# Slot sums for two sequences per matmul, and a reordered end of the token phase, in a recurrence-plus-soft-MoE kernel

## The chip, the cores and the metric

One core of a Trainium2 chip runs the whole program. Its engines work side by side, each on its own queue of instructions: TensorE (PE; its weight loads are shown as PEld) multiplies matrices into the accumulation memory (PSUM), VectorE (DVE) and ScalarE (ACT) work elementwise and copy out of PSUM, GpSimd (POOL) works elementwise on on-chip memory and issues the weight loads, and SyncE (SP) issues the other transfers. The metric is the device time of one execution in microseconds; lower is better. Times are given as the median of several executions.

## The reference

Four sequences of 5056 tokens with 256 channels go through a gated recurrence, and all 20224 tokens together through a soft mixture of eight experts with four slots each.

```python
# recurrence, per sequence
sig = 1.0 / (1.0 + np.exp(-f_logit))
f = lower_bound + (1.0 - lower_bound) * sig
h = f[:, t] * h + (1 - f[:, t]) * x[:, t]        # y[:, t] = h, for each t
# soft MoE over all tokens of all sequences, x = y
logits = x @ phi                                 # (20224, 32)
d = softmax of logits over the tokens
slot_input = d.T @ x                             # (32, 256)
h = np.maximum(slot_input[e] @ w1[e], 0.0)       # per expert e, its 4 slots
slot_out[e] = h @ w2[e]
c = softmax of logits over the 32 slots
out = c @ slot_out                               # (20224, 256)
```

The slot inputs need every token of every sequence, so no output can leave before the last token has been through the recurrence, the logits and the experts.

## The kernel before

**Token phase.** A sequence is cut into ten groups of up to 512 tokens (group 8, which the code calls `odd`, has 448; group 9 is `last`). One group of one sequence is a unit; there are 40, numbered n. For a unit, SyncE loads f_logit and x; ScalarE takes the sigmoid (`gate`, L249); GpSimd multiplies by x (`enter`, u_t, L260); TensorE transposes both to channels by rows (sp, up: L264, L271, L277, L300); ScalarE makes the decay (a, L315 and L322); VectorE scans along the tokens (h, L333); TensorE turns h back to tokens (`to_tokens`, hp, L346); and VectorE or ScalarE keeps that in ht (`keep_tokens`, L365). When all four sequences have a group, TensorE makes the logits (lg, L379), ScalarE their exponentials (`exps`, L388), TensorE transposes these (L400) and a copy keeps them as et (L403), and TensorE adds up the slot inputs (`slots`, L430).

**Slot sums.** The sums stand in one half of one PSUM bank, 128 partitions (4 sequences x 32 slots) by 256 channels. For a group, `slots` issues 16 matmuls (4 rows r x 4 sequences b), each with 32 columns of weights (et) and 256 moving columns (ht), and sequence b has its own 32 partitions. The sums for groups 0 to 7 are issued inside the loop, those for group 8 (L430) and group 9 (`late_slots`, L475) after it.

**Unread matmuls.** The other half of that bank takes `idle` matmuls (L194, in fp32, 128 columns of weights, 256 moving columns), issued at set places in the loop; nothing reads them. `spin` (L157) and `narrow` (L162, 32 columns of weights) are others, into other PSUM space, at the end of the token phase and among the experts.

**What sets the order.** The program's order is written by hand; every engine goes through its own instructions in that order. Waits between engines follow from the tiles: an instruction waits for the earlier instructions that wrote, or read, the tile it reads or writes. Transfers of experts' weights are issued on GpSimd's queue at set units (`W_AT`), the last six at n = 36; the w2 of the last two experts goes into a buffer (w_t, L152) that held f_logit.

**End of the token phase.** At n = 39 the logits of group 8 are finished for the last sequence, then come its exponentials, the slot sums of group 7, the transposes of group 8's weights (`odd_weights`, L469, copied by ScalarE, L470) and the scan of the last unit. After the loop: the last logits of group 9, `late_exps` (L454), hp and ht of the last unit, `late_weights` (L461, copied by VectorE, L462), the slot sums of groups 8 and 9, one copy of the sums to slot_sb (L614), and a matmul that adds the four sequences' 32 rows (L618). late_ps and odd_ps lie in one PSUM tile (tail).

**Experts and outputs.** The slot inputs go through w1 (L649), are turned (L664), and then through w2 (sum_ps, L688, for experts 0 to 6). Among experts 4 to 6 TensorE also adds each token's exponentials over the slots (`row_sums`, L413, into tail), whose reciprocals VectorE takes (rrow, L739). The last expert has its own form (so_ps, sb_ps, L748), and then slot_out (L760) is there and the output phase begins: matmuls (op, L788, L841), a scaled copy by VectorE or ScalarE (L778, L782), and stores.

Of the kernel before, what the change touches and what calls it, by code (L numbers as in the profile page):

```python
# [18 lines left out]
def kernel(  # L19
# [10 lines left out]
    nc = tc.nc  # L30
    B, S, D = x.shape
    E = moe_w1.shape[0]
    F = moe_w1.shape[2]
    NS = moe_phi.shape[1]
    SPE = NS // E
    P = 128
    DC = D // P
    FC = F // P
    R = 4
    G = P * R  # L40
    n_grp = (S + G - 1) // G
    n_unit = n_grp * B
# [12 lines left out]
    odd = n_grp - 2  # L55
# [12 lines left out]
    ident_f = consts.tile([P, P], F32, name="ident_f")  # L68
# [104 lines left out]
    with tc.tile_pool(name="sp2", bufs=3) as sp2, \  # L173
# [7 lines left out]
         tc.tile_pool(name="pslot", bufs=1, space=PSUM) as pslot:  # L181

        slot_bank = pslot.tile([P, 2, D], F32, name="slot_ps")
        slot_ps = slot_bank[:, 0]

        wide_rep = rep.rearrange("p b s -> p (b s)").unsqueeze(1).broadcast_to([P, 2, P])

        def idle(k, first=False):
            if first:
                for i in range(2):  # L190
                    nc.tensor.matmul(slot_bank[:, 1, ds(0, P)], ident, ident,
                                     start=True, stop=False, skip_group_check=True)
            for _ in range(k):
                nc.tensor.matmul(slot_bank[:, 1], ident_f, wide_rep,  # L194
                                 start=False, stop=False, skip_group_check=True)
        xs, fs, sts, uts, pss, psus, hs, hps, hts, lgs, ets = ({} for _ in range(11))

# [158 lines left out]
        def keep_tokens(n):  # L356
            g, b = place(n)
            n_p = rows(g)
            by_scalar = n % 2 and n >= SINGLE - 2
            if 2 * B < n < n_unit - 2 * B and n % (2 * B) in (1, B):  # L360
                by_scalar = not by_scalar
            if n in (n_unit - 8, n_unit - 4):
                by_scalar = True
            copy = nc.scalar.copy if by_scalar else nc.vector.tensor_copy
            copy(hts[g][:n_p, b].rearrange("p r d -> p (r d)").bitcast(F32),  # L365
                 hps.pop(n)[:n_p].rearrange("p r c -> p (r c)"))
# [58 lines left out]
        def slots(g):  # L425
            n_p = rows(g)
            et, ht = ets.pop(g), hts.pop(g)
            for r in range(R):
                for b in range(B):
                    nc.tensor.matmul(slot_ps[ds(b * NS, NS), :], et[:n_p, r, b],  # L430
                                     ht[:n_p, b, r],
                                     start=(g == 0 and r == 0),
                                     stop=(g == n_grp - 1 and r == R - 1),
                                     skip_group_check=True)

        def unit(f, m):
# [27 lines left out]
        def odd_weights():  # L464
            n_p = rows(odd)
            ets[odd] = etok.tile([P, R, B, NS], BF16, name="et", tag="et")
            ew = etall[:, ds(first(odd), n_p * R)].rearrange("s (p r) -> s p r", r=R)
            for r in range(R):
                nc.tensor.transpose(odd_ps[:n_p, r], ew[:, :, r], ident)  # L469
            nc.scalar.copy(ets[odd][:n_p].rearrange("p r b s -> p r (b s)"), odd_ps[:n_p])  # L470

        def late_slots():
            for r in range(R):
                for b in range(B):
                    nc.tensor.matmul(slot_ps[ds(b * NS, NS), :], ets[last][:, r, b],  # L475
                                     hts[last][:, b, r],
                                     start=False, stop=r == R - 1,
                                     skip_group_check=True)

        AHEAD = 6  # L480
        SETTLED = 3 * B
# [17 lines left out]
        for n in range(n_unit):  # L499
            if n < SINGLE - 2:  # L500
                if n:
                    unit(to_tokens, n - 1)
                    unit(u_to_channels, n + 1)
                s_to_channels(n + 2)
                if n + 3 < SINGLE:
                    gate(n + 3, 1)
                decay(n + 2, 1)
                if n + 3 == SINGLE:
                    gate(n + 3)
                if n % 2 == 0:  # L510
                    unit(load, n + AHEAD)
                unit(enter, n + 3)
                rep_constants(n)
            else:
                end = n >= n_unit - 6
                if n % 2 == 0:
                    unit(load, n + AHEAD)
                    if n == SINGLE - 2:
                        to_tokens(n - 1)
                        keep_tokens(n - 1)  # L520
                    if n >= SETTLED:
                        unit(gate, n + 4)
                else:
                    unit(decay, n + 1)
                    if seven(n) and place(n)[1] % 2 == 0:
                        nc.scalar.copy(uts[n + 2][:, R - 1], uts[n][:, R - 1])
                    if n < SETTLED:
                        gate(n + 3)
                    if n == n_unit - 5:
                        exps(odd - 1)  # L530
                if not end and n != n_unit - 7:
                    group(exps, n - 2)

                unit(enter, n + 3)
                for _ in range(W_AT.get(n, 0)):
                    load_w(w_next[0])
                    w_next[0] += 1

                late = seven(n)
                if n != SINGLE - 2 and not late:  # L540
                    unit(to_tokens, n - 1)
                if late:
                    unit(u_to_channels, n + 1)
                    unit(to_tokens, n - 1)
                if n == n_unit - 2:
                    keep_tokens(n - 1)
                if n % 2 == 0:
                    unit(s_to_channels, n + 2)
                    unit(s_to_channels, n + 3)
                if not late:  # L550
                    unit(u_to_channels, n + 1)
                if n == SINGLE - 2:
                    idle(1, True)
                elif late and n in (n_unit - 7, n_unit - 5, n_unit - 3):
                    idle(1)
                elif not late and n % (2 * B) in (1, 5, 6, 7):
                    idle(2 if n in (6, 7) else 1)
                if n == n_unit - 2:
                    tail = psp.tile([P, 2, G], F32, name="tail", tag="sp")
                    sums = tail[:, 0]  # L560
                    rs_ps = sums[:, ds(0, n_grp * R * B)].rearrange(
                        "p (q b) -> p q b", b=B)
                    late_ps, odd_ps = (
                        tail[:, 1].bitcast(BF16)[:, ds(i * R * P, R * P)].rearrange(
                            "p (r s) -> p r s", r=R) for i in range(2))
                    logits(odd, [0, 1, 2])
                    logits(last, [0, 1, 2])
                    slots(odd - 2)
                elif not end and long(n - 1):
                    if n % B == 0:  # L570
                        g = (n - 1) // (2 * B) * 2
                        for i in range(2):
                            logits(g + i, [2, 3] if n % (2 * B) == 0 else [0, 1])
                elif not end:
                    group(logits, n - 1)
            if n == n_unit - 1:
                logits(odd, [3])
                exps(odd)
                slots(odd - 1)
                odd_weights()  # L580

            unit(scan, n)
            if n not in (SINGLE - 2, n_unit - 2):
                unit(keep_tokens, n - 1)
            if n == n_unit - 3:
                weights_to_tokens(odd - 1, nc.scalar.copy)
            elif not n >= n_unit - 6:
                group(weights_to_tokens, n - 3)
                batch(slots, n - 4, 0)
                batch(slots, n - 4, 1)  # L590
                if n > 2 * B and n % (2 * B) == 3:
                    idle(1)
# [10 lines left out]
        late_exps()  # L603
        left_over()
        to_tokens(n_unit - 1)
        keep_tokens(n_unit - 1)
        late_weights()
        slots(odd)
        late_slots()
        spin(tail[:, 1], 2, D)  # L610
        narrow(tail[:, 1], 10)
        slot_sb = hpool.tile([P, G, DC], BF16, name="slot_sb", tag="h")
        slot_sb = slot_sb.rearrange("p t o -> p (t o)").bitcast(F32)[:, ds(0, D)]
        nc.vector.tensor_copy(slot_sb, slot_ps)  # L614
        sin_ps = tail[:, 0, ds(G // 2, DC * NS)].rearrange("p (o s) -> p o s", o=DC)
        slot_v = slot_sb.rearrange("p (c o) -> p o c", o=DC)
        for o in range(DC):
# [5 lines left out]
    with tc.tile_pool(name="ew", bufs=1) as ew, \  # L623
# [108 lines left out]
        for i in range(len(blocks)):  # L732
            expert(Q + i)
            row_sums(i)
            if i < 2:
                narrow(tail[:, 1], 34, NS)
            if i < len(blocks) - 1:
                k = ds(i * wide_r, wide_r)
                nc.vector.reciprocal(rrow[:, k], rs_ps[:, k])  # L739
# [166 lines left out]
```

## Time and profile before

| | |
|---|---|
| Time, median of 3 runs | 198.06 us (198.0 to 199.38) |
| The profiled execution's own time | 197.88 us |
| Its span, first to last instruction | 196.1 us |
| Mean TensorE clock granted | 0.877 of full speed |
| TensorE busy | 150.4 us (77%), 1328 matmuls |
| VectorE busy | 144.2 us (74%) |
| ScalarE busy | 142.6 us (73%) |
| GpSimd busy | 101.2 us (52%) |
| HBM read, written | 58.23 MB, 20.71 MB |

The profile comes from one execution. Its page cuts the span into 40 equal slices (4.9 us each) and gives, for each, the busy share of each engine in tenths, the granted TensorE clock in tenths and the share of the 16 DMA engines. A timeline row reads: start in us from the span's beginning, duration, engine, line, operation, what is written and read, shapes (rows*columns of the array in use, then partitions x elements), how many in a row, and in brackets how long the engine had been idle and what released it. Rows of a chain of waits are pieces of the path that ended last: start, duration, engine, tile and line. Matmuls are pipelined, so the durations of neighbours overlap, and a row of several is shorter than their sum.

### The profile page before, as it was taken

To read this page: it belongs to the slowest core of one execution; us is meant where nothing else is said; L and a number is where in the kernel's file an instruction comes from. 1 tells how busy PE (TensorE), PEld (TensorE's weight loads), DVE (VectorE), ACT (ScalarE), POOL (GpSimd) and SP (SyncE) were. 2 spreads that over 40 slices of the span, in tenths; PEclk is the share of its full clock that TensorE was granted. 3 is DMA by queue.
4 is the path that set the end of the run, shared out by engine and by line. 5 is a ranking of instruction groups with operands and counts; after the bars stand their busy time and mean duration, and the time that the engine had idled before them with its cause. 6 is when DMAs were issued, how large, how long until landed. Compare 5 with 4: busy or idle time off the path is not lost.

```text
span 196.1 us, 3514 instructions
## 1 busy us (share of the span) xinstructions
PE 150.4 (77%) x1328; PEld 104.7 (53%) x1328; DVE 144.2 (74%) x187; ACT 142.6 (73%) x202; POOL 101.2 (52%) x78
## 2 busy tenths in 40 slices
PE   0687579888979979897999998999899999930000
PEld 0475458676756858665786776648674434300000
DVE  3669789999899999999989999333377998920000
ACT  3688678899689999899986898425089999950000
POOL 2689586894988588894989995270030000000000
PEclk9999999999999999999999999999995555555555
DMA  5999999999999999999999999999749999999994
GB/s 209 419 419 419 433 428 423 428 424 340 399 424 421 398 346 423 428 424 322 407 422 409 241 212 215 214 215 211 133 166 428 420 434 424 428 434 438 448 434 177
DMA packets 13010, 70.77 MB, mean 361 GB/s; under 512 B 1457, under 2 KB 2738, under 8 KB 9026
## 3 DMA queue, kind: packets, MB, share of 16 engines
q1 hardware_dynamic: 10368, 62.13, 76.0%
q0 software_dynamic: 2624, 8.42, 21.6%
q8 instruction: 10, 0.16, 0.3%
q14 instruction: 6, 0.05, 0.1%
q10 hardware_dynamic: 2, 0.00, 0.0%
HBM read 58.23 MB, written 20.71 MB: 403 GB/s over the span
## 4 chain that ended last, share of the span: by engine, by line
PE 39%; DMA 22%; DVE 13%; ACT 7%; POOL 5%; issue 3%; POOLq 1%; ACTq 0%; SPq 0%
DMA x_t<-in_x_dram 14%; DVE h L333 9%; PE op L841 9%; DMA f_t<-in_f_logit_dram 7%; PE hp L346 5%; PE up L271 5%; POOL u_t L260 4%; ACT oc L782 3%; PE sp L264 2%; PE sp L271 2%; DVE ht L365 2%; PE lg L379 2%; PE op L788 2%; PE slot_ps L194 2%; PE tail L413 1%
## 5 line engine op out<-in xcount | busy, mean ns | idle before, releaser
L260 POOL TENSOR_TENSOR u_t<-s_t,x_t 128x1024 bf16<-128x1024 bf16 (+1 forms) x39 | 82.4, 2127 | 20.7 <-ACT s_t L249 11.3
L333 DVE TENSOR_TENSOR_SCAN h<-a,h,up 128x512 bf16<-128x512 f32 (+1 forms) x72 | 86.6, 1251 | 3.6 <-PE up L271 2.5
L249 ACT ACTIVATE s_t<-f_t 128x2048 bf16<-128x2048 f32 (+2 forms) x23 | 38.3, 1669 | 7.0 <-DMA f_t<-in_f_logit_dram 7.0
L346 PE MATMUL hp<-ident_f,h 128*128 128x128 f32 (+1 forms) x160 | 29.0, 304 | 5.8 <-DVE ht L365 3.9
L346 PEld LDWEIGHTS hp<-ident_f,h 128*128 128x128 f32 (+1 forms) x160 | 23.1, 206 | 13.9 <-DVE ht L365 7.8
L315 ACT ACTIVATE a<-sp,lbs 128x1024 f32<-128x1024 bf16 x24 | 25.4, 1114 | 0.6 <-PE sp L264 0.6
L271 PE MATMUL up<-ident_f,u_t 64*128 64x64 f32 x248 | 23.1, 229 | 2.7 <-POOL u_t L260 2.5
L782 ACT ACTIVATE oc<-op,rrow 128x256 f32<-128x256 f32 x62 | 24.4, 508 | 0.2
L264 PE MATMUL sp<-ident_f,s_t 128*128 128x128 f32 x128 | 19.1, 292 | 6.8 <-ACT s_t L249 4.5
L841 PE MATMUL op<-slot_bd,etall 64*128 64x512 bf16 x62 | 23.3, 584 | 0.5 <-POOL slot_bd L771 0.3
L271 PEld LDWEIGHTS up<-ident_f,u_t 64*128 64x128 f32 x248 | 18.1, 138 | 7.9 <-POOL u_t L260 3.4
L322 ACT ACTIVATE a<-sp,lbs 128x512 f32<-128x512 bf16 (+1 forms) x22 | 18.2, 875 | 5.4 <-PE sp L264 3.1
L778 DVE TENSOR_TENSOR oc<-op,rrow 128x512 f32<-128x512 f32 x31 | 19.9, 684 | 1.9 <-PE op L841 1.9
L264 PEld LDWEIGHTS sp<-ident_f,s_t 128*128 128x128 f32 x128 | 15.3, 150 | 8.7 <-ACT s_t L249 5.0
L194 PE MATMUL slot_ps<-rep,ident_f 128*128 128x256 f32 x48 | 15.7, 416 | 1.0 <-POOL rep L88 1.0
L841 PEld LDWEIGHTS <-etall 64*128 64x128 bf16 x62 | 9.0, 153 | 13.4 <-issue 7.9
L365 DVE COPY ht<-hp 128x512 f32<-128x512 f32 (+1 forms) x20 | 13.4, 671 | 2.2 <-PE hp L346 2.2
L365 ACT COPY ht<-hp 128x512 f32<-128x512 f32 (+1 forms) x20 | 11.7, 583 | 2.8 <-PE hp L346 2.8
L333 DVE TENSOR_TENSOR_SCAN h<-a,up 128x512 bf16<-128x512 f32 x8 | 9.3, 1208 | 2.5 <-ACT a L322 1.7
L379 PE MATMUL lg<-h,phi 128*32 128x512 bf16 (+1 forms) x80 | 10.1, 390 | 0.0
L194 PEld LDWEIGHTS slot_ps<-rep,ident_f 128*128 128x128 f32 x48 | 7.3, 188 | 2.8 <-POOL rep L88 1.2
L430 PE MATMUL slot_ps<-ht,et 128*32 128x256 bf16 (+1 forms) x144 | 8.6, 276 | 0.0
(131 smaller groups left out, 147.7 us busy)
## 6 DMA issues: line engine op xcount, KB each, us to landing
f_t<-in_f_logit_dram SPq DMA_DIRECT2D x12, 1024.0 KB, 13.0
x_t<-in_x_dram SPq DMA_DIRECT2D x12, 1024.0 KB, 12.1
out_dram<-oc SPq DMA_DIRECT2D x6, 2048.0 KB, 13.5
w_sb<-in_moe_w_dram POOLq DMA_DIRECT2D x14, 512.0 KB, 10.4
f_t<-in_f_logit_dram SPq DMA_DIRECT2D x8, 512.0 KB, 9.2
x_t<-in_x_dram SPq DMA_DIRECT2D x8, 512.0 KB, 8.8
f_t<-in_f_logit_dram SPq DMA_DIRECT2D x4, 896.0 KB, 13.0
x_t<-in_x_dram SPq DMA_DIRECT2D x4, 896.0 KB, 11.7
```

The costliest lines, as they stand in the source:

```text
L194: nc.tensor.matmul(slot_bank[:, 1], ident_f, wide_rep, start=False, stop=False, skip_group_check=True)
L249: nc.scalar.activation(s_t, f_t, ACT.Sigmoid, scale=-1.0)
L260: nc.gpsimd.tensor_tensor(uts[n][:, :r], s_t[:, :r], x_t[:, :r], ALU.mult)
L264: nc.tensor.transpose(ps[:, :, r], t(n % 2 * R + r).bitcast(F32), ident_f)
L271: nc.tensor.transpose(v[:, :, r], t(r)[k].bitcast(F32), ident_f[k, k])
L315: nc.scalar.activation(a, sp[:, :, :, :, o], ACT.Identity, scale=nomlb[:, ds(o, 1)], bias=1.0)
L333: nc.vector.tensor_tensor_scan(h[:, :T, o], decays[n // 2, o][:, n % 2, :T], up[:, :T, o], hs[number(g - 1, b)][:, ds(used(g - 1) - 1, 1), ...
L346: nc.tensor.transpose(hp[:n_p, r], hw[:, :n_p, r], ident_f)
L365: copy(hts[g][:n_p, b].rearrange("p r d -> p (r d)").bitcast(F32), hps.pop(n)[:n_p].rearrange("p r c -> p (r c)"))
L778: nc.vector.tensor_tensor(ob, op, scale.broadcast_to(list(ob.shape)), ALU.mult)
L782: nc.scalar.activation(ob[:, i], op[:, i], ACT.Copy, scale=scale[:, i])
L841: nc.tensor.matmul(op.rearrange("p u d -> p (u d)"), ew[:, :, r], slot_bd[ds(j * 2 * NS, 2 * NS)].rearrange("s u d -> s (u d)"), start=Tru ...
```

## The change

`slots` takes two sequences at once for groups 0 to 6: 64 columns of weights (the et of both) and 512 moving columns (the ht of both), eight matmuls a group instead of 16. The output fills 64 partitions by the whole bank. The blocks on the diagonal are the sums wanted (an even sequence in the first half of the bank, an odd one in the second); the other two blocks mix two sequences and aren't read. Groups 7, 8 and 9 still take one sequence at a time, into the half that belongs to it. `late_slots` is replaced by `slots(last)`, which does the same work.

Since the bank is now full, `idle` writes only a block that isn't read, 32 partitions of the second half: it has 32 columns of weights instead of 128. The three idle matmuls at n = 33, 35 and 37 go. The sums are copied to slot_sb in four pieces of 32 partitions, by VectorE and ScalarE in turn, each from the half that holds its sequence.

`odd_weights` moves from n = 39 to behind `to_tokens` of the last unit, so the last logits come ahead of it on TensorE, and `late_exps` ahead of its copy on ScalarE. The last unit's ht copy goes from ScalarE to VectorE. The two runs of 34 `narrow` matmuls among the experts go. No transfer changes, and GpSimd's and SyncE's queues keep their order.

```diff
         slot_bank = pslot.tile([P, 2, D], F32, name="slot_ps")
-        slot_ps = slot_bank[:, 0]
...
-                    nc.tensor.matmul(slot_bank[:, 1, ds(0, P)], ident, ident,
+                    nc.tensor.matmul(slot_bank[ds(0, NS), 1, ds(0, P)], ident[:, ds(0, NS)], ident,
                                      start=True, stop=False, skip_group_check=True)
             for _ in range(k):
-                nc.tensor.matmul(slot_bank[:, 1], ident_f, wide_rep,
+                nc.tensor.matmul(slot_bank[ds(0, NS), 1], ident_f[:, ds(0, NS)], wide_rep,
                                  start=False, stop=False, skip_group_check=True)
...
             if n in (n_unit - 8, n_unit - 4):
                 by_scalar = True
+            if n == n_unit - 1:
+                by_scalar = False
...
         def slots(g):
             n_p = rows(g)
             et, ht = ets.pop(g), hts.pop(g)
+            k = 2 if g < odd - 1 else 1
             for r in range(R):
-                for b in range(B):
-                    nc.tensor.matmul(slot_ps[ds(b * NS, NS), :], et[:n_p, r, b],
-                                     ht[:n_p, b, r],
-                                     start=(g == 0 and r == 0),
-                                     stop=(g == n_grp - 1 and r == R - 1),
+                for b in range(0, B, k):
+                    dst = slot_bank if k == 2 else slot_bank[:, b % 2]
+                    nc.tensor.matmul(dst[ds(b * NS, k * NS)],
+                                     et[:n_p, r, ds(b, k)].rearrange("p b s -> p (b s)"),
+                                     ht[:n_p, ds(b, k), r] if k == 2 else ht[:n_p, b, r],
+                                     start=g == 0 and r == 0,
+                                     stop=g == n_grp - 1 and r == R - 1,
                                      skip_group_check=True)
...
-        def late_slots():
-            for r in range(R):
-                for b in range(B):
-                    nc.tensor.matmul(slot_ps[ds(b * NS, NS), :], ets[last][:, r, b],
-                                     hts[last][:, b, r],
-                                     start=False, stop=r == R - 1,
-                                     skip_group_check=True)
...
-                elif late and n in (n_unit - 7, n_unit - 5, n_unit - 3):
-                    idle(1)
                 elif not late and n % (2 * B) in (1, 5, 6, 7):
                     idle(2 if n in (6, 7) else 1)
...
                 exps(odd)
                 slots(odd - 1)
-                odd_weights()
...
         to_tokens(n_unit - 1)
+        odd_weights()
         keep_tokens(n_unit - 1)
         late_weights()
         slots(odd)
-        late_slots()
+        slots(last)
...
-        nc.vector.tensor_copy(slot_sb, slot_ps)
+        for b in range(B):
+            k = ds(b * NS, NS)
+            (nc.scalar.copy if b % 2 else nc.vector.tensor_copy)(slot_sb[k], slot_bank[k, b % 2])
...
             row_sums(i)
-            if i < 2:
-                narrow(tail[:, 1], 34, NS)
```

## The prediction

> **What bounds the kernel now.** I began with the page's 40 slices: which resource never rests, and where it does.
>
> ```profile
> PEclk9999999999999999999999999999995555555555
> DMA  5999999999999999999999999999749999999994
> ```
>
> The DMA engines are full from the first loads to slice 27 and again from slice 30; the clock falls to half only with the outputs. Between 140 and 145 us DMA rests (share 0.37 in 140 to 142, 0.11 in 142 to 145). So the time is: loads and weights until about 142, a gap, then 20.71 MB of outputs at about 430 GB/s, 48 us that nothing shortens. What counts is when the first output leaves, and that needs the last expert's w2 and the slot sums. The timeline there, and the issues of that w2 (tile w_t, POOL's queue):
>
> ```profile
> 119.64 0.54 POOL L152 DMA_DIRECT2D w_t<-in_moe_w_dram  x1 [0.43 <-DMA w_sb<-in_moe_w_dram]
> 127.06 0.53 POOL L152 DMA_DIRECT2D w_t<-in_moe_w_dram  x1 [1.91 <-DMA w_sb<-in_moe_w_dram]
> ...
> 141.41 0.60 PE L748 MATMUL so_ps<-w_t,hid 128*128 128x256 bf16 x4
> 141.94 0.11 PEld L748 LDWEIGHTS <-hid 128*128 128x128 bf16 x2 [0.22 <-DMA w_t<-in_moe_w_dram]
> ```
>
> Four issues take 15.5 to 19.4 us to land: the 256 KB part 122.10 + 19.3 = 141.4, the last 128 KB 127.06 + 15.5 = 142.6. TensorE starts L748 at 141.41 and waits again at 141.94. Its weights for L748 were loaded from 141.17, so it stands ready some 0.1 us before the part. Compute and weights finish together: **work taken out ahead of L748 can gain almost nothing, work put in is paid in full** once some 0.2 us of waiting (0.1 here, 0.1 at 141.94) is used up.
>
> Next, the chain of waits back from there. From 56 us it is compute, changing between VectorE's scans and stretches of TensorE; these pieces (start, us) are touched:
>
> ```profile
> 75.45 0.63 PE slot_ps L194 x2
> 76.08 0.47 PE hp L346 x4
> ...
> 96.31 0.54 PE slot_ps L430 x11
> 96.84 0.68 PE hp L346 x4
> ...
> 122.59 0.54 PE slot_ps L430 x12
> ```
>
> L430 is a slot sum of a group, L194 an idle matmul.
>
> **The change part by part**, on the profiled run's own 197.88 us (span 196.1; the median of the three runs is 198.06, 0.2 above).
>
> *Pairs, groups 0 to 6.* Sixteen 32-column, 256-wide matmuls become eight 64-column, 512-wide. The sixteen took 0.53 to 0.55 us on the chain, so four quarters of the array run at once. Eight on two halves are four waves of 512; the logits, also 512 wide and two abreast there, go at 0.23 a wave (chain, 73.13 and 73.37). 4 x 0.23 = 0.92, so +0.38 a group. Groups 0, 1, 2 and 4 run where TensorE then waits for VectorE or loads (after 68.6 it waits until 70.3), so those are covered; without that cover they cost 0.38 each. Groups 3, 5 and 6 (73.6, 96.3, 122.6) are on the chain: **+1.15**. No 64-column matmul is in this trace. Bounds: 0 if it goes as before; if halves don't overlap, a 512-wide one after another costs 0.25 (L841, 1.72 for 7 at 145.58), 8 x 0.25 - 0.55 = +1.4 a group, 4.3 in all. I take the waves, since every 32-column group here overlaps.
>
> *Idle matmuls with 32 columns.* Streaming stays 256 wide. But hp, 0.47 after L194, is 0.68 after L430 or the 64-row transposes: a change of tile shape costs 0.2. The narrow idle brings that change. Three lie on the chain (58.0, 75.5, 98.2): **+0.6**. Below, shorter weight loads (0.11 between its two loads) could give back 0.1 each, -0.3; above, a second change, +1.2. The nearest row is hp's. [...]
>
> *Three late idles gone.* At 109.0 the transposes behind it wait for ScalarE's u_t copy (109.09 to 109.49); at 113.4 ScalarE is busy from 112.74 to 117.2 and sets the pace; at 118.4 TensorE waits afterwards until 120.12. All beside the path: 0 (bounds -1.2, thrice 0.43, to 0).
>
> *Group 8's weights later.* The tail of before:
>
> ```profile
> 125.01 0.63 PE L469 MATMUL tail<-ident,etall 128*112 128x128 bf16 x4 [0.29 <-ACT etall L388]
> 125.57 0.62 PE L379 MATMUL lg<-h,phi 128*32 128x512 bf16 x2
> 125.67 0.59 ACT L470 COPY et<-tail 112x512 bf16<-112x512 bf16 x1 [0.72 <-PE tail L469]
> 126.12 0.75 PE L346 MATMUL hp<-ident_f,h 128*128 128x128 f32 x4
> 126.23 0.60 ACT L454 ACTIVATE etall<-lg 128x512 bf16<-128x512 f32 x1
> 126.97 0.41 PE L461 MATMUL tail<-ident,etall 128*128 128x128 bf16 x4
> 128.65 0.42 DVE L614 COPY slot_sb<-slot_ps 128x256 f32<-128x256 f32 x1 [0.73 <-PE slot_ps L475]
> 129.28 0.55 PEld L618 LDWEIGHTS tail<-rep,slot_sb 128*128 128x128 f32 x4 [0.21 <-DVE slot_sb L614]
> ```
>
> In the changed program the last logits wait for group 8's exponentials (one lg tile), and group 9's transposes wait for ScalarE's copy of group 8's (one tail tile). So: exponentials done 124.96; logits 125.0; hp 0.55 later, 125.56; group 8's transposes 0.68 later, 126.24, about 0.5; copy 126.8 to 127.4; group 9's transposes 127.4 instead of 126.97. **+0.4**: the logits gain 0.55 and the copy that had been beside them moves onto the path. The last ht copy, 0.6 on ScalarE, goes to VectorE (0.69 for such a copy) at about 126.35, ahead of its next work: covered; uncovered 0.1. Behind the waiting transposes stand both groups' slot sums and all that follows. If the tile waits cost nothing, -0.55; above, +0.6.
>
> *Four copies of slot_sb.* 32 rows by 256 each, VectorE and ScalarE in turn, and in the built program each waits for the one before, the matmul L618 for the last. A 32x256 VectorE copy took 0.40 (L717), a 128x256 ScalarE one 0.41 (L756): rows fewer, no time saved. 0.06 + 0.42 + 0.41 + 0.42 + 0.41 + three hand-overs of 0.04 + 0.05 = 1.89 from the last slot sum (128.59) to L618; it was 0.69. **+1.2**. Bounds: 0.25 each (L630's 128x32) +0.5; ScalarE at 0.76 (L700, 32x256) +1.9.
>
> *No unread matmuls among experts.*
>
> ```profile
> 135.98 1.22 PE L413 MATMUL tail<-ones,etall 128*128 128x128 bf16 x16
> 137.12 0.41 PE L162 MATMUL tail<-w_sb 128*32 128x32 bf16 x34
> 137.62 0.56 DVE L739 RECIPROCAL rrow<-tail 128x64 f32<-128x64 f32 x1 [2.46 <-PE tail L162]
> ```
>
> The reciprocal waits for the 34, and the next row sums (138.23) for the reciprocal. Without them it starts at 137.27 and the row sums at 137.88: -0.35, twice, **-0.7** (bounds -0.8, the 0.41s, to 0).
>
> Sum at L748: 1.15 + 0.6 + 0.4 + 1.2 - 0.7 = 2.65, less the 0.2 of waiting: +2.45. SP's and POOL's queues keep their order; loads land about 12 us after issue, so DMA doesn't starve meanwhile. **197.88 + 2.45 = 200.3 us.**
>
> **Rivals.** *Not slower: the last w2 stays late.* Decided at L748: while compute is under 0.2 us later there, 142.6 still sets the end. It needs VectorE to cover the pairs and shape changes (it is 90% busy or more in most slices from 12 to 22) and copies of 32 rows at L630's 0.25: 0.4 + 0.5 - 0.7 = 0.2, so 197.9. Against it: the chain names TensorE at those places, and L717. Up to 198.9 if part holds. Faster than that it can't be; the weights land when they land.
>
> *The clock drops before the outputs.* Mean clock is 0.79 in 145 to 150, with TensorE busy 4.51 of 5.00 us, and 0.50 in 150 to 155, busy 5.00: being busy doesn't hold it. There the matmuls use 64 or 32 rows. If the used area counts, idles with a quarter of the columns hold it less, as do late idles and experts' fillers left out. L841 went from 0.25 to 0.43 us each, so a TensorE stretch like 120.1 to 124.3 would take 2 to 3 us more: about 202.5, up to 205 with two. For it: so many fillers are cut at once. Against: from 120 to 142, mostly 32-column work, clock 1.00, and the pairs double the area. [...]
>
> *Halves that don't overlap*: 4.3 for 1.15, 203.4.
>
> **How the numbers follow.** Forecast 0.45 (199.4 to 201.2), not slower 0.21, clock 0.20, no overlap 0.14. The range 198.4 to 203.4 leaves about 0.1 below and 0.1 above: the bounds of the copies and shapes move the end by under 1, those of the pairs make the last rival. 1% (2 us) is about what this kernel's measurement tells from no change; over 200.04 lie two thirds of the forecast and both dear rivals: slower 0.62, same 0.34, faster 0.04.
>
> **What would show it.** Four slot_sb copies in a row, 1.7 us or more; slot sums of 0.9 us; group 9's transposes over 2 us after group 8's exponentials; L748 reached after w2 has landed, with no wait for DMA; outputs as full as now. I am wrong if a wait for w_t still stands before L748, or if PEclk shows less than full before slice 30.

## The result and the profile after

The changed kernel takes **204.36 us** (median of four executions, 202.44 to 204.59) against 198.13 us for the kernel before on the same chip: a ratio of 1.0279, 95% interval 1.0203 to 1.0354. Measured once more beside another set of executions of the kernel before, it took 202.94 us against 199.06, ratio 1.0209 (1.0127 to 1.0291). The forecast was 200.3 us. The profiled execution took 204.15 us, with a span of 202.4 us, 6.3 longer than before. In the page's 40 slices (5.06 us each; the granted clock, then the DMA share):

```profile
PEclk9999669996999999999999995899999655555555
DMA  6999999999999999999999999999019999999994
```

Before, the clock was full in every slice up to the outputs. Here it is at half in three more places: 21.8 to 28.7 us (slices 4 and 5), 45.7 to 49.2 (slice 9) and 120.8 to 127.7 (slices 23 to 25). DMA rests longer ahead of the outputs: two slices at 0 and 1 tenth, where before the lowest were 7 and 4.

The end of the token phase and the first matmuls on w2, from the timeline:

```profile
134.61 0.41 DVE L610 COPY slot_sb<-slot_ps 32x256 f32<-32x256 f32 x1 [0.73 <-PE slot_ps L433]
135.06 0.36 ACT L610 COPY slot_sb<-slot_ps 32x256 f32<-32x256 f32 x1 [2.14 <-DVE slot_sb L610]
135.45 0.42 DVE L610 COPY slot_sb<-slot_ps 32x256 f32<-32x256 f32 x1 [0.43 <-ACT slot_sb L610]
135.91 0.36 ACT L610 COPY slot_sb<-slot_ps 32x256 f32<-32x256 f32 x1 [0.49 <-DVE slot_sb L610]
136.32 0.55 PEld L614 LDWEIGHTS tail<-rep,slot_sb 128*128 128x128 f32 x4 [1.28 <-ACT slot_sb L610]
...
147.68 0.60 PE L742 MATMUL so_ps<-w_t,hid 128*128 128x256 bf16 x4
```

The four copies stand one behind the other. L742 (L748 before; line numbers shift by up to six between the two kernels) begins at 147.68, 6.27 us later than before, and carries no wait: the last w2 landed at 143.4. So compute sets the end, as the forecast had it, and the 6.3 us of the span are all there before the first output.

Pieces of the chain of waits (start, us, what; L433 is a slot sum here, L193 an idle matmul, L345 hp):

```profile
46.44 1.85 PE slot_ps L433 x8
48.29 0.99 PE slot_ps L193 x2
...
75.85 0.98 PE slot_ps L433 x8
76.84 0.68 PE hp L345 x4
...
78.15 0.55 PE slot_ps L193 x2
78.70 0.68 PE hp L345 x4
```

Eight paired matmuls take 0.98 us at full clock (sixteen single ones took 0.54) and 1.85 at half. After an idle, hp now takes 0.68 instead of 0.47, while the idle (L193) takes 0.55 instead of 0.63.

### The profile page after: what moved, and what is told of

Same layout as the page of the kernel before. It is cut to its first block, busy times and chain, and to the rows that moved or that the text cites. A ratio compares the mean times of both kernels' runs of the same rounds, so it can differ in the third digit from the quotient of the medians.

```text
span 202.4 us, 3257 instructions
## 1 busy us (share of the span) xinstructions
PE 157.0 (78%) x1198; PEld 102.4 (51%) x1198; DVE 144.9 (72%) x189; ACT 142.6 (70%) x203; POOL 101.3 (50%) x78
## 4 chain that ended last, share of the span: by engine, by line
PE 43%; DVE 15%; DMA 10%; ACT 10%; POOL 6%; issue 3%; SPq 1%; POOLq 1%; ACTq 0%
DVE h L332 10%; PE op L835 8%; PE hp L345 7%; DMA x_t<-in_x_dram 7%; PE up L270 5%; POOL u_t L259 5%; ACT oc L776 5%; PE sp L263 4%; PE slot_ps L433 4%; DMA f_t<-in_f_logit_dram 3%; PE lg L380 3%; DVE ht L366 3%; PE sp L270 2%; ACT a L321 2%; PE slot_ps L193 2%
## 5 line engine op out<-in xcount | busy, mean ns | idle before, releaser
L248 ACT ACTIVATE s_t<-f_t 128x2048 bf16<-128x2048 f32 (+2 forms) x23 | 38.3, 1669 | 3.3 <-DMA f_t<-in_f_logit_dram 3.3
L345 PE MATMUL hp<-ident_f,h 128*128 128x128 f32 (+1 forms) x160 | 31.0, 320 | 4.6 <-DVE ht L366 4.1
L345 PEld LDWEIGHTS hp<-ident_f,h 128*128 128x128 f32 (+1 forms) x160 | 23.0, 208 | 18.2 <-DVE ht L366 9.5
L263 PE MATMUL sp<-ident_f,s_t 128*128 128x128 f32 x128 | 20.0, 302 | 6.6 <-ACT s_t L248 4.4
L776 ACT ACTIVATE oc<-op,rrow 128x256 f32<-128x256 f32 x62 | 24.3, 540 | 0.2
L835 PE MATMUL op<-slot_bd,etall 64*128 64x512 bf16 x62 | 22.7, 570 | 0.6 <-ACT oc L776 0.2
L263 PEld LDWEIGHTS sp<-ident_f,s_t 128*128 128x128 f32 x128 | 16.3, 156 | 8.3 <-ACT s_t L248 4.7
L366 DVE COPY ht<-hp 128x512 f32<-128x512 f32 (+1 forms) x21 | 14.1, 672 | 5.5 <-PE hp L345 5.5
L366 ACT COPY ht<-hp 128x512 f32<-128x512 f32 (+1 forms) x19 | 11.1, 585 | 8.4 <-PE hp L345 8.4
L193 PE MATMUL slot_ps<-rep,ident_f 128*32 128x256 f32 x42 | 13.5, 413 | 0.0
L380 PE MATMUL lg<-h,phi 128*32 128x512 bf16 (+1 forms) x80 | 12.1, 443 | 0.3 <-ACT etall L389 0.3
L433 PE MATMUL slot_ps<-ht,et 128*64 128x512 bf16 (+2 forms) x104 | 10.5, 353 | 0.0
L765 POOL TENSOR_SCALAR slot_bd<-slot_out,parity 128x256 bf16<-128x256 bf16 x2 | 1.8, 918 | 16.7 <-DVE slot_out L754 16.7
```

Of the source, the lines that this page charges most:

```text
L248: nc.scalar.activation(s_t, f_t, ACT.Sigmoid, scale=-1.0)
L263: nc.tensor.transpose(ps[:, :, r], t(n % 2 * R + r).bitcast(F32), ident_f)
L345: nc.tensor.transpose(hp[:n_p, r], hw[:, :n_p, r], ident_f)
L776: nc.scalar.activation(ob[:, i], op[:, i], ACT.Copy, scale=scale[:, i])
L835: nc.tensor.matmul(op.rearrange("p u d -> p (u d)"), ew[:, :, r], slot_bd[ds(j * 2 * NS, 2 * NS)].rearrange("s u d -> s (u d)"), start=Tru ...
```

## The experiments

Fifteen more runs were made, two of them of the unchanged kernels. Each is compared with executions of the kernel before on its own chip in the same session; over all sessions those took 197.9 to 201.1 us, with medians from 198.0 to 199.3. That spread is itself a finding, below. "Early drop" is half clock before 60 us, "late drop" half clock between 118 and 128 us. All these kernels compute the whole reference.

| kernel | median us | beside it, before | ratio (95%) | half clock in its profile, ahead of the outputs |
|---|---|---|---|---|
| before, again | 198.96 | 198.92 | 1.0001 (0.9966 to 1.0037) | 22.5-26.0, 118.1-121.5 |
| before, 32-column idles | 198.98 | 199.32 | 1.000 (0.996 to 1.004) | 22.7-26.1 |
| before, no late idles | 201.42 | 199.32 | 1.011 (1.004 to 1.018) | 22.7-26.1, 118.3-125.1 |
| before, only n = 33, 35 | 201.06 | 198.40 | 1.0145 (1.0077 to 1.0213) | 22.8-26.2, 118.3-125.2 |
| before, only n = 37 | 199.74 | 198.40 | 1.0061 (1.0014 to 1.0108) | 45.0-48.5 |
| before, no narrow | 199.32 | 199.32 | 0.9992 (0.996 to 1.0024) | 21.6-28.5, 45.5-48.9 |
| before, four copies | 199.74 | 199.06 | 1.0039 (0.9997 to 1.0081) | 22.9-26.4 |
| before, late idles doubled | 198.68 | 199.06 | 0.9986 (0.995 to 1.0021) | 21.9-28.8, 45.8-49.3 |
| before, more idles | 199.68 | 199.06 | 1.0026 (0.999 to 1.0061) | 58.2-61.7 |
| after, again | 202.94 | 199.06 | 1.0209 (1.0127 to 1.0291) | 23.7-27.2, 119.3-126.1 |
| after, late idles back | 201.35 | 198.92 | 1.0146 (1.0088 to 1.0204) | 24.0-27.5 |
| after, only n = 37 back | 202.26 | 197.99 | 1.0204 (1.0139 to 1.0268) | 22.8-26.3 |
| after, quadrant idles | 203.19 | 199.32 | 1.0187 (1.0107 to 1.0267) | 34.9-38.3 |
| after, no pairs | 199.88, the others 203.21 to 203.34 | 198.92 | none | 24.5-31.4, 120.1-126.9 |
| after, no pairs, late idles back | 200.10 | 198.92 | 1.0073 (1.0043 to 1.0103) | 24.3-27.8 |

The first theory was that the clock fell because the idles use a quarter of the columns, early and late alike. The next four sections test it.

### The kernel before with narrow idles

```diff
-                nc.tensor.matmul(slot_bank[:, 1], ident_f, wide_rep,
+                nc.tensor.matmul(slot_bank[ds(0, NS), 1], ident_f[:, ds(0, NS)], wide_rep,
```

> The kernel before, with one part of the change: the idle matmuls have 32 columns of weights and write 32 partitions; all of them stay, the three at n = 33, 35, 37 too. Theory 1 (the width of the idles decides the clock early): the granted clock shows less than full near 22 to 29 us and 46 to 49 us, as in the changed kernel, and the time is 2.0 to 2.6 us over the kernel before (there the scan's h at 60.7 us came 2.26 later). Rival (the early drops came from the pairs or by chance of phase): the clock stays full up to the outputs, and the time is 0.3 to 0.6 us over, for the changes of tile shape alone. If the late idles too need their width, a drop near 120 us comes on top: 3.5 to 4.5 over.

Measured: 198.98 against 199.32 us, ratio 1.000 (0.996 to 1.004). Its clock:

```profile
PEclk9999889999999999999999999999996555555555
```

One short early drop, and full from 26.1 us to the outputs. Theory 1 falls at its centre: the width of the idles costs no time that shows, and doesn't make the late drop.

### The kernel before without the late idles

```diff
-                elif late and n in (n_unit - 7, n_unit - 5, n_unit - 3):
-                    idle(1)
```

> The kernel before without the three idle matmuls at n = 33, 35 and 37; nothing else. Theory 1 (they hold the clock over the end of the token phase): the clock drops to half near 117 to 124 us for some 7 us, and the time is 1.5 to 2 us over the kernel before (hp, lg and the last slot sums at half clock lost about 1.7 in the changed kernel). Rival (they lay beside the path and hold nothing; the late drop follows from the narrow idles before): full clock, time within 0.2.

Measured: 201.42 us, 2.1 over the kernel before beside it (by the interval 0.8 to 3.6). Its clock:

```profile
PEclk9999789999999999999999985999995555555555
```

The late drop is there, 118.3 to 125.1 us, with nothing changed but three matmuls of 0.4 to 0.6 us that nobody reads. This part of the theory stands.

### The changed kernel with idles that fill the array

```diff
+            for _ in range(4 * k):
+                for b in range(B):
+                    nc.tensor.matmul(slot_bank[ds(b * NS, NS), 1 - b % 2], ident[:, ds(0, NS)],
+                                     wide_id, start=False, stop=False, skip_group_check=True)
...
+                elif late and n in (n_unit - 7, n_unit - 5, n_unit - 3):
+                    idle(1)
```

> The changed kernel, with idles that fill the array again: each idle is four rounds of four bf16 matmuls of 32 columns and 256 moving, one for each block of the bank that is not read, so all 128 columns are in use for about as long; and the three idles at n = 33, 35, 37 are back. Pairs, four copies, reordered end and no narrow matmuls among the experts stay. Theory 1 (used columns of the idles hold the clock): full clock up to the outputs, and the time falls from 204.2 to 199.9 to 200.6 us, the forecast without the clock's part. Rival (the pairs, or the narrow matmuls left out, lower the clock): drops stay, 203 to 204.5.

Measured: 203.19 us. The time lies in the rival's range, but the profile fits neither: the late drop is gone and the clock is full from 38.3 us to the outputs, but there is a drop at 34.9 to 38.3, and the scans that were 0.7 us ahead of the kernel before at 28 us are 2.9 behind at 39. In that stretch TensorE waits 1.64 us for GpSimd (u_t) and then goes at half clock. So this profile speaks for the late idles, and not the pairs, as what decides the late drop; since these idles are themselves another load, it says nothing on the rest.

### The kernel before without the narrow matmuls

```diff
-            if i < 2:
-                narrow(tail[:, 1], 34, NS)
```

> The kernel before without the two runs of 34 narrow matmuls among the experts. Theory (the last w2 sets the end, so work taken out ahead of it gains almost nothing): 0 to 0.2 us faster, and a longer wait for w_t ahead of L748. Rival 1: 0.6 to 0.8 us faster, if the outputs follow the compute alone. Rival 2: slower by 1 us or more, if these matmuls hold the clock over the first outputs.

Measured: 199.32 against 199.32 us, as the theory had it, though the interval (0.996 to 1.0024) alone would still allow rival 1's 0.6 to 0.8. What decides is this row of its timeline, ahead of the outputs (its L746 is L748 of the kernel before):

```profile
141.84 0.60 PE L746 MATMUL so_ps<-w_t,hid 128*128 128x256 bf16 x4 [0.42 <-DMA w_t<-in_moe_w_dram]
```

TensorE waits 0.42 us for w2: work taken out ahead of it gains nothing. The bound that the prediction began with is shown. The unlooked-for thing is its clock:

```profile
PEclk9999669996999999999999999999995555555555
```

Up to 136 us this program is that of the kernel before. Its early drops, 21.6 to 28.5 and 45.5 to 48.9, are those of the changed kernel within 0.3 us. So they are not the change's doing. And they cost little here: scans are 0.9 us later than in the first profile at 46 us, 0.7 from 72 to 121. In the same stretch of its chain:

```profile
46.24 0.98 PE slot_ps L430 x12
47.22 1.15 PE slot_ps L194 x2
```

The single slot sums that fall under half clock take 0.98 us, where the pairs took 1.85.

This made theory 2: early drops come and go between executions; the late one hangs on the late idles.

### Both kernels once more, and the late idles put back

The kernel before and the changed one, unchanged:

> The kernel before, unchanged, profiled once more. In the kernel without narrow matmuls, whose program is the same up to 136 us, the clock fell to half at 21.6 to 28.5 and 45.5 to 49.0 us, where the one profile of the kernel before shows it full. Theory 2 (the early drops come and go from execution to execution, whatever the change): a drop before 60 us in this profile too or in some of its executions, and times that spread from 198 to 200.5. Rival (without the change's idles no early drop): full clock to 147.9 us, 198.0 to 198.4.

> The changed kernel, unchanged, profiled once more. Theory 2 (the late drop belongs to the change, the early ones come and go): half clock near 118 to 127 us again; the early drops elsewhere or fewer. Its executions spread from about 202.3 (one early drop or none) to 204.6. Rival (the late drop too comes and goes): full clock from 50 us to the outputs in this profile, 201.5 or less.

The changed kernel with its late idles:

```diff
+                elif late and n in (n_unit - 7, n_unit - 5, n_unit - 3):
+                    idle(1)
```

> The changed kernel with the three idles at n = 33, 35 and 37 put back, 32 columns wide as its other idles; nothing else. Theory 2 (the presence of these idles holds the clock at 118 to 127 us, their width does not matter, as it did not in the kernel before with narrow idles): full clock from 118 us to the outputs, 1.6 to 2.1 us below the changed kernel, 202.3 to 202.8. Rival (in the changed kernel they must fill the array): the late drop stays, 204 to 204.6.

The kernel before, again: 198.96 us, executions from 198.03 to 200.63, and a profile that isn't full:

```profile
PEclk9999789999999999999999996999996555555555
```

It has an early drop, and a short late one of 3.4 us too. So the one profile that the prediction rested on was an execution without drops, and theory 2's first half stands. The changed kernel again, with a lone short early drop and the late drop of 6.8 us:

```profile
PEclk9999879999999999999999985999999655555555
```

With its late idles back it took 201.35 us, 2.4 below the changed kernel (203.75, median of its eight executions in two other sessions). Its clock:

```profile
PEclk9999979999999999999999999999996555555555
```

These last two profiles have the same early drop, within 0.3 us, and so can be laid side by side. The chain of the changed kernel, again:

```profile
121.59 0.47 PE up L276
122.07 0.94 PE up L270 x7
123.01 1.06 PE hp L345 x4
124.07 1.72 PE lg L380 x12
125.79 1.16 PE slot_ps L433 x8
126.95 0.63 PE hp L345 x4
```

The chain with the late idles back:

```profile
121.93 0.33 PE up L276
122.26 0.58 PE up L270 x7
122.83 0.68 PE hp L345 x4
123.51 0.96 PE lg L380 x11
124.48 0.98 PE slot_ps L433 x8
125.46 0.63 PE hp L345 x4
```

The same six pieces: 5.99 us from first to last against 4.16, so 1.83 lost. Without the idles the first piece starts 0.34 us earlier, but 0.19 of that stands already at 105 us (105.39 against 105.58), ahead of the first late idle. So leaving them out gave back 0.15, although the chain with them names two (at 110.87 and 115.32): 1.7 us net. The first output leaves at 148.36 against 146.84 us.

### The pairs

```diff
-            k = 2 if g < odd - 1 else 1
+            k = 1
```

> The changed kernel with the slot sums of every group taken one sequence at a time, 16 matmuls of 32 columns and 256 moving; bank halves, four copies, narrow idles and the rest stay. Theory 2 (each group's pairs on the path cost 0.4 to 0.5 us at full clock, and one of them 1.3 where the clock is half): 1.6 to 2.6 us below the changed kernel, 201.8 to 202.8. Rival (the forecast's term as it stood): 1.15 us, 203.2. Second rival (the pairs cover the array and hold the clock): more drops, 204 or more.

> The changed kernel with both: one sequence at a time, and the three late idles back. What is left of the change: 32-column idles, four copies, the reordered end, no narrow matmuls among the experts. Theory 2 (the parts add up): the kernel before plus 0.1 to 0.3 (idles) plus 1.04 (copies) plus 0.36 (order) less 0.77 (narrow matmuls) less up to 0.2 of waiting, 0.5 to 1.0 over the kernel before run beside it. Rival (something not yet named remains in the bank's two halves or in the order): 2 us or more over it.

Without pairs, and without the late idles: one execution took 199.88 us at a mean clock of 0.879, the other three 203.21 to 203.34 at 0.849; the profile is of one of these and has drops at 24.5 to 31.4 and 120.1 to 126.9. Executions so far apart give no price for the pairs. They show what the drops can make of one program. At 0.879 there seems to have been no drop ahead of the outputs (the first profile of the kernel before has 0.877 with none), and 199.88 us is no more than the 199.96 that the next kernel, with the late idles, took at 0.880. So leaving the late idles out makes the late drop frequent, not certain, and without a drop it costs nothing that shows.

With the late idles back the two kernels differ in the pairs alone: 201.35 against 200.10 us, 1.25 for the pairs, where 1.15 was forecast; the two intervals leave about 1.3 either way. Against the kernel before, 1.2 us (0.9 to 2.0) remain, a little over the 0.5 to 1.0 expected. In its profile 1.25 us of delay stand already at the seventh scan (18.80 us against 17.55), which the parts left in don't explain; from the last scan to L748's matmuls it takes 0.6 us more than the kernel before, as the terms for the order, the copies and the narrow matmuls make it.

### Four copies alone

```diff
-        nc.vector.tensor_copy(slot_sb, slot_ps)
+        for b in range(B):
+            k = ds(b * NS, NS)
+            (nc.scalar.copy if b % 2 else nc.vector.tensor_copy)(slot_sb[k], slot_ps[k])
```

> The kernel before with slot_sb copied in four pieces of 32 partitions, by VectorE and ScalarE in turn; nothing else. Theory (the copies are on the path, 1.04 us as in the changed kernel's profile, less up to 0.2 in which w2 is awaited anyway): 0.8 to 1.05 us over the kernel before. Rival 1 (they run beside each other, a piece costs a quarter): 0 to 0.2. Rival 2 (the forecast's 1.2 stands): 1.2 to 1.4.

Measured: 199.74 against 199.06 us, +0.7 with an interval from 0 to 1.6, so the times exclude neither rival. The trace does exclude rival 1: it has 128.79 to 130.50 us from the first copy to the weights of the matmul behind (L618 before), 1.71 where one copy took 0.63: +1.08, and a piece of 32 rows costs as much as the whole:

```profile
128.79 0.41 DVE L616 COPY slot_sb<-slot_ps 32x256 f32<-32x256 f32 x1 [0.73 <-PE slot_ps L475]
129.23 0.36 ACT L616 COPY slot_sb<-slot_ps 32x256 f32<-32x256 f32 x1 [1.60 <-DVE slot_sb L616]
```

### More idles in the kernel before

```diff
                 elif late and n in (n_unit - 7, n_unit - 5, n_unit - 3):
-                    idle(1)
+                    idle(2)
```

> The kernel before with two idle matmuls instead of one at n = 33, 35 and 37; nothing else. Theory 2 (what TensorE does at 109 to 118 us decides the clock at 118, and the kernel before is near the edge, since one of its profiles shows half clock from 118.1 to 121.6): no late drop, its slowest executions rarer, median 0.2 to 0.6 us below the kernel before beside it. Rival (the second idle lands on the path): 0.4 to 1.2 us over it. If neither, the same within 0.3.

```diff
             if n < SINGLE - 2:
...
                 rep_constants(n)
+                if n >= 2:
+                    idle(2, n == 2, wide_id)
...
                 if n == SINGLE - 2:
-                    idle(1, True)
+                    idle(2, False, wide_id)
...
-                elif not late and n % (2 * B) in (1, 5, 6, 7):
+                elif not late and (n % (2 * B) in (1, 5, 6, 7) or n in (10, 11)):
```

> The kernel before with two late idles for one as in the run beside it, and with idles where the early drops follow: two at n = 2, 3 and 4 (identity as the moving operand) and one at n = 10 and 11. Theory 2 (an early drop follows a stretch in which TensorE rests, 18 to 22 and 42 to 45 us): clock full up to the outputs, median 198.0 to 198.4, below the kernel before at 198.9 to 199.3. Rival 1 (the early idles come too late or the drops have another cause): drops stay, as the kernel before. Rival 2 (the idles lengthen the path): 199.5 to 200.5 with the clock full.

The second has the doubled late idles too. Neither beats the kernel before: 0.9986 (0.995 to 1.0021) and 1.0026 (0.999 to 1.0061). With more idles early the drops at 22 and 45 us are gone from the profile and one stands at 58.2 to 61.7 instead; the scan that began at 63.62 us begins at 65.33. With one profile of each, and early drops that come and go, these runs don't show whether the filling moved the drop.

### Which late idle

```diff
-                elif late and n in (n_unit - 7, n_unit - 5, n_unit - 3):
+                elif late and n == n_unit - 3:
```

> The kernel before with only the late idle at n = 37 (118.4 us); those at n = 33 and 35 (109.0 and 113.4 us) are out. Theory 3 (the clock at 118 us is decided by the TensorE work of the 3 to 7 us before it): half clock from about 118 for 7 us, 1.5 to 2.2 us over the kernel before. Rival (the idle inside the stretch holds it): full clock there, within 0.3.

```diff
-                elif late and n in (n_unit - 7, n_unit - 5, n_unit - 3):
+                elif late and n in (n_unit - 7, n_unit - 5):
```

> The kernel before with the late idles at n = 33 and 35 (109.0 and 113.4 us); the one at n = 37 (118.4 us) is out. Theory 3 (the clock at 118 us is decided before it): as the kernel before, within 0.3, the late drop no longer or more frequent than there. Rival (the idle inside the stretch holds it, or ends it early): half clock from about 118 to 125, 1.5 to 2.2 us over the kernel before.

Theory 3, that the clock is decided by the work ahead of the drop, falls. With the idles at n = 33 and 35 alone the kernel is as slow as with none (201.06 us) and has the long late drop:

```profile
PEclk9999789999999999999999995899995555555555
```

With n = 37 alone the profile has no late drop, and the time is 199.74, 1.2 over the kernel before (0.3 to 2.1). That is more than the rival's 0.3, so the other two may do something; what, these runs don't show.

How the one at n = 37 acts is seen where the drop began at the same place. Stretches of the kernel before, again (length, then busy time and count of PE, PEld, DVE, ACT, POOL, then the clock, DMA share and GB/s):

```profile
118.10:121.50 3.40, 3.38 (x19) 2.78 (x20) 3.08 (x3) 3.29 (x5) 1.95 (x4) 0.50 1.07 217
121.50:125.00 3.50, 3.50 (x57) 2.42 (x56) 2.79 (x3) 1.07 (x2) 0.79 (x2) 1.00 1.05 210
```

Its timeline in the first of them:

```profile
119.03 1.06 PE L194 MATMUL slot_ps<-rep,ident_f 128*128 128x256 f32 x2
119.88 1.06 PE L400 MATMUL ep<-ident,etall 128*128 128x128 bf16 x8
120.73 0.42 PE L277 MATMUL up<-ident_f,u_t 128*128 128x128 f32 x1
```

The same stretches with n = 33 and 35 alone:

```profile
118.10:121.50 3.40, 2.94 (x19) 2.38 (x20) 3.10 (x3) 3.40 (x5) 1.98 (x4) 0.54 1.07 216
121.50:125.00 3.50, 3.50 (x33) 1.94 (x34) 2.45 (x2) 0.90 (x2) 0.81 (x2) 0.50 1.05 210
```

And its timeline:

```profile
118.99 1.06 PE L400 MATMUL ep<-ident,etall 128*128 128x128 bf16 x8
120.46 0.47 PE L277 MATMUL up<-ident_f,u_t 128*128 128x128 f32 x1 [0.41 <-ACT u_t L526]
```

Both fall to half at 118.1 to 118.3. With the idle, TensorE is busy 3.38 of the 3.40 us that follow, and the clock is back at 121.5; without it TensorE waits 0.41 us for ScalarE, is busy 2.94, and stays at half for as long again, under the logits, slot sums and hp of the chain. So in these two profiles the idle cuts the drop short; it doesn't prevent it.

### That one idle in the changed kernel

```diff
+                elif late and n == n_unit - 3:
+                    idle(1)
```

> The changed kernel with one line more: the idle at n = 37 is back, 32 columns wide; those at n = 33 and 35 stay out. Theory 4 (this one alone cuts the late drop): at most 3.4 us of half clock between 118 and 128 us where the changed kernel has 6.8 in both its profiles, and 1.5 to 2.5 us below it, 201.0 to 202.0. Rival (all three are needed in the new order): 6.8 us of half clock there, 202.5 to 204.5.

Its profile has no half clock between 26.3 us and the outputs:

```profile
PEclk9999789999999999999999999999998555555555
```

That execution took 200.97 us, the median is 202.26 (200.97 to 202.85; ratio 1.0204, 1.0139 to 1.0268). For the clock theory 4 held in this profile. The time is above its range; the other three executions had a mean clock of 0.859 to 0.860 against 0.874 here, and where theirs dropped isn't known.

## Why the prediction was wrong

**What bounds the kernel.** Right. w2 and compute finish together in the kernel before, so that less work gains nothing (0.9992 without the narrow matmuls), and later compute is paid in full (no wait at 147.68).

**The sum.** Its terms came out near. Three pairs on the chain cost 0.98 - 0.55 = 0.43 each, 1.3 in all (1.15 forecast; 1.25 by the medians): four waves, as worked out. The logits ahead of them take another 0.1 each. The narrow idles cost 0.13 each, 0.4 (0.6): hp pays 0.21 behind the narrow idle (0.68 for 0.47), and the idle gives 0.08 back (0.55 for 0.63). The other order costs 0.3 from the last scan to the first copy (0.4), by the kernel without pairs. The copies cost 1.04 (1.2), the narrow matmuls gave 0.77 back (0.7). In the kernel with the late idles back, L748's matmuls start at 144.38 against 141.41 us; 0.33 of that was there at the scans near 73 us, after its early drop, and 2.64 came since. That the forecast's terms before waiting add up to 2.65 is partly luck: one of its three idles on the chain lies ahead of 73 us, so the terms as measured give 2.1 behind it, and the rest came in pieces that it didn't name, 0.3 of it at the logits and 0.1 at the late idles. By the medians this kernel is 2.4 us over the one before. A change that kept those idles would have landed where the forecast put this one, but for the early drops that both kernels have.

**The step that failed** is that of the three late idles: "All beside the path: 0 (bounds -1.2, thrice 0.43, to 0)". The reading of the path was nearly right: the chain of the kernel before does name two of them (0.43 us each, at 109.21 and 113.53), but their removal gave back only 0.15 us. What it lacked is what they do to the clock. Without them the clock is at half for 6.8 us from 118 to 121 on in both profiles of the changed kernel, in that without pairs, and in both kernels before that lack n = 37; that stretch cost 1.83 us where it could be laid beside a kernel with full clock. The times put the idles at 2.1 us in the kernel before (0.8 to 3.6) and about 2.4, across sessions, in the changed one.

**The clock as a rival** had a chance of 0.20 and 202.5 us for one drop. It was the case that came about, and its price for one drop (2 to 3 us) was near. Of the three causes that it named, all under used area, the runs bear out one, the late idles left out. Narrow idles leave the time as it is, and without the experts' fillers no drop came between 128 us and the outputs. What was held against it, full clock from 120 to 142 us in the one profile, was weak evidence: the same program was at half from 118.1 to 121.5 when profiled again. The sign it named for being wrong, "if PEclk shows less than full before slice 30", was the right row.

**The rest of the 6.3 us** of the profiled pair is partly the draw. The first profile of the kernel before had no early drop; this one of the changed kernel had 10 us of them. Up to 46 us the kernel without narrow matmuls ran with the same clock: there the drops cost 0.7 us that lasted. Beyond them the changed kernel lost another 1.3 us between 46 and 57 us: 0.87 where a group's pairs (1.85 for 0.98) fell under half clock, and some 0.5 at the next group's pairs and logits, at full clock and on the chain in both executions. The prediction counted such groups as covered by VectorE or loads; that cover holds at full clock (0.3 us from 46 to 55 us with the late idles back, given back by 73 us) and not at half.

*No overlap of 64-column halves* (203.4) and *not slower* (197.9) are both excluded by rows: 0.98 us for eight, and no wait for w2.

What stays open: what exactly the clock follows. A small busy share over such a stretch is not it alone. In the same view of stretches, the kernel before with n = 37 alone kept the full clock with TensorE busy less:

```profile
118.10:121.50 3.40, 2.66 (x24) 2.18 (x25) 3.18 (x4) 3.40 (x5) 1.95 (x4) 1.00 1.06 213
```

## What to carry to other kernels

A matmul that nobody reads had two prices here: its place on the path, which a profile shows (0.43 us for each of two late idles; in the changed kernel 0.15 came back without the three), and what it does to the granted clock, which showed only when it was gone (2.1 us in the kernel before, 0.8 to 3.6); take such matmuls out alone before counting them as free. One profile with a full clock is one draw (the kernel before had no half clock ahead of the outputs in its first profile, and twice 3.4 us in its second): profile the same program twice before leaning on PEclk. And a piece that a wait covers at full clock can come onto the path when the clock halves (here a group's pairs, 1.85 us for 0.98), so bulky work beside a stretch that sometimes drops is dearer than it looks.

## What the runs showed of the hardware

- **The late drop came without a long rest ahead of it.** In the kernel before, profiled again, TensorE was busy 9.72 of the 10.20 us from 107.9 to 118.1 us, where the clock fell, and its two waits in the last 5 us of that were 0.23 and 0.26.
- **Half clock lasted 3.4 or 6.8 us** in all the drops ahead of the outputs (6.83, 3.41 and 6.83 in the first profile of the changed kernel), and started at another place in each execution (21.6 to 24.5 us for the first in most). Within one execution the measured starts lie whole multiples of 3.41 us apart, to within 0.1: 21.85, 45.74, 120.84 and, at the outputs, 158.38 us in the changed kernel (7, 22 and 11 of them); 95.5 to 95.6 us (28) in the five profiles of the table that have a drop before 25 and one at 118 to 121 us; 23.9 us (7) in the two with drops at 22 and 45 us. What decides where they lie, and whether the clock falls, is not shown.
- **The width of the unread matmuls showed no effect on it.** Idles of 32 columns for 128 left the time the same (ratio 1.000, 0.996 to 1.004); with idles filling the four quadrants the one profile still has an early drop, 34.9 to 38.3 us.
- **A copy of 32 partitions cost as much as one of 128**: VectorE 0.41 us against 0.42 for 256 channels. ScalarE took 0.36 for such a piece; no run has it copy the whole. Two engines on four pieces, in turn, took 1.71 us to the next matmul's weights where one copy took 0.63.
- **Two 64-column halves ran beside each other**: eight matmuls of 512 columns in 0.98 us, where eight one after another would take an estimated 2.0 (L841 of the kernel before took 1.72 for seven).
